# A gated linear-attention and feed-forward kernel: the last stage's steps in another order

## The chip, the cores and the metric

The kernel runs on one core of one Trainium2 chip. The metric is the device time of one execution in microseconds (us), here as the median of several runs. Beside it stands one profiled execution, whose trace gives the start and duration of every instruction on the engines PE (matrix), DVE (vector), ACT (scalar), POOL (GpSimd) and on the DMA queue that SP (SyncE) feeds.

## The reference

The input `x` has 2048 rows of 640 values. Two branches are computed from it and mixed row by row with a sigmoid gate.

```python
x = A_x
g = _sigmoid((x * gate_w).sum(-1, keepdims=True))
# branch A: 32 heads of 20; q, k, v from x @ wqkv
pq = einsum("bhsd,hdf->bhsf", q, w_phi);  pk = einsum("bhsd,hdf->bhsf", k, w_phi)
phi_q = concat([softmax(pq), softmax(-pq)]);  phi_k = concat([softmax(pk), softmax(-pk)])
kv = einsum("bhsf,bhsd->bhfd", phi_k, v);  z = einsum("bhsf->bhf", phi_k)
num = einsum("bhqf,bhfd->bhqd", phi_q, kv);  den = einsum("bhqf,bhf->bhq", phi_q, z) + 1e-6
a = (num / den) @ wo
# branch B: dense
b = silu(x @ w1) @ w2
return g * a + (1 - g) * b
```

## The kernel before

Products are made from operands that are split in a high part and a low part (`split`: ACT rounds a tile into its high part, then DVE or POOL subtracts it from the original), so most matrix products are three passes, listed in `PASSES`. The work is in three stages.

Stage 1 computes keys and values of 16 row tiles of 128 and sums `kv` and `z`. Stage 2 is the dense branch, in four blocks of 512 rows; its results, times 1 - g, go to the DRAM buffer `fb_d` (`acc_mm` is the last products of one of five output chunks, `acc_out` the DVE product into a tile `o` and its store). At the end of stage 2 the first four query tiles (rows 1536 to 2047) are already processed up to their feature maps. Stage 3, the last stage, handles the rest of the queries and all outputs. It works on eight pairs of tiles (256 rows), in the order `PB`; a pair is called u = 0 to 7.

For one query tile t the functions are, in order:

- `q_mm`: 30 matmuls project the tile into PSUM (`pq`).
- `q_logits`: DVE takes maximum and minimum of each head and subtracts (lines 410, 411 and twice 417), then ACT takes the exponential of 128x1280 values (line 776, tile `eq`).
- `q_norm`: POOL multiplies `eq` by the broadcast `z` (line 790, tile `ez`). `q_sum`: DVE sums `eq` over each head (line 780).
- `q_norm_sum`: DVE sums `ez` (line 793). `q_small`: five small instructions make the weights of each head from both sums and the gate (lines 801 to 820; DVE, for the first four tiles partly POOL).
- `q_mul`: POOL multiplies `eq` by these weights (line 826).

For a pair u: `t_all` transposes both tiles' `eq` on PE (line 963, `pT`) and copies them with ACT to `fT`; `n_mm` multiplies by the `kv` weights (line 1033, `pn`), three matmul groups; `n_out` makes the high part on ACT and the low part on DVE (`oT`); `w_mm(u, m0, n)` loads the dense result from `fb_d` into a tile `y` and multiplies `oT` by `wo` (line 1071, `pa`); `w_out` adds `y` and stores to `out`. Adding is done from a copy: ACT copies `pa` to `pac` (`w_copy`, line 1083), POOL adds (line 1094). For the last pair DVE adds straight from PSUM (line 1096). The five output chunks of a pair are taken in three groups, (0, 2), (2, 2) and (4, 1).

The transposes, `pn` and `pa` share four PSUM banks in turn (`single`), so a group waits until what stood in its bank four groups earlier is copied out. `pq` has two PSUM tiles of its own; they lie where the dense branch's banks were.

The inputs of stage 3's tiles come in 18 pieces (three per pair: 128x512, 128x512, 128x256). `x_next(k)` splits the next k pieces (ACT cast, then POOL subtract, both recorded with line 120 or 122) and issues the load of the piece four further on (line 216, tile `xrb`). The loads share four buffers, so piece p + 4 is loaded only when piece p is split.

Step u of stage 3 (function `step`, u = 1 to 6) handles the query tiles numbered a = 2u - 2, b = 2u - 1 and c = 2u; tiles a and b together are pair u + 1, which the next step transposes. In the first step a is tile 0, b is tile 1, c is tile 2. `inorder(PE, DVE, ACT, POOL)` around the stage makes the order in which the calls are written the order on each of these engines. SP's order of loads and stores is set by the scheduler from the order of the program. After the six steps `last_steps` transposes pair 7 and finishes the outputs of pairs 6 and 7.

Of the kernel before, what the change touches and what calls it, by code (L numbers as in the profile page):

```python
# [25 lines left out]
NP = S // 256  # L26
# [35 lines left out]
def mix_kernel(ctx: ExitStack, tc: tile.TileContext, xT, wqT, wkc, wkr, wv, bd, bdc, cst, wo, w1, w1r, w2, out):  # L62
# [729 lines left out]
    def q_norm_sum(t):  # L792
        nc.vector.tensor_reduce(Q[t]["sm"][:, 2 * H : 4 * H], groups(Q[t]["ez"]), axis=AX.X, op=ALU.add)  # L793

    def q_parts(t):

        s, sm = sums[t], Q[t]["sm"]
        w, parts = sm[:, 2 * H : 4 * H], halves(sm[:, 4 * H : 6 * H])
        first, other = halves(w)[:, :, 0], halves(s)[:, :, ::-1]
        if t // 4 == NB - 1:  # L800
            nc.gpsimd.tensor_tensor(first, sm[:, 4 * H : 5 * H], first, op=ALU.add)
            nc.gpsimd.tensor_tensor(parts, halves(w), other, op=ALU.mult)
        else:
            nc.vector.scalar_tensor_tensor(first, halves(s)[:, :, 0], 1e-6, first, op0=ALU.mult, op1=ALU.add)
            nc.vector.tensor_tensor(parts, halves(w), other, op=ALU.mult)

    def q_inv(t):
        sm = Q[t]["sm"]
        r = sm[:, :H]
        nc.vector.tensor_reduce(r, halves(sm[:, 4 * H : 6 * H]), axis=AX.X, op=ALU.add)  # L810
        nc.vector.reciprocal(r, r)

    def q_weights(t):
        s, sm = sums[t], Q[t]["sm"]
        w = sm[:, 2 * H : 4 * H]
        rb = sm[:, :H][:, :, None].to_broadcast([P, H, 2])
        if t // 4 == NB - 1:
            nc.gpsimd.tensor_tensor(halves(w), halves(sm[:, 6 * H :])[:, :, ::-1], rb, op=ALU.mult)
        else:
            nc.vector.scalar_tensor_tensor(  # L820
                halves(w), halves(s)[:, :, ::-1], g[:, t : t + 1], rb, op0=ALU.mult, op1=ALU.mult
            )
# [160 lines left out]
    with inorder(PE, DVE, ACT, POOL):  # L983
        q_open(t, q_proj(t))
        q_norm(t - 1)
        xb_split(2)
        acc_mm(0)
        q_feat(t)
        q_norm_sum(t - 1)
        q_parts(t - 1)  # L990
        acc_out(0)
        q_inv(t - 1)
        q_weights(t - 1)
        q_mul(t - 1)
        q_sum(t)
        q_norm(t)
        acc_mm(1)
        acc_out(1)
        acc_mm(2)
        acc_out(2)  # L1000
        for i in range(4):
            t_mm(0, i, bank)
            t_out(0, i)
        q_norm_sum(t)
        q_parts(t)
        acc_mm(3)
        acc_out(3)
        q_inv(t)
        q_weights(t)
        q_mul(t)  # L1010
        acc_mm(4)
        acc_out(4)

    closed("psf", "fp")
    tb = opened("tb", reuse_waits="tile")
# [68 lines left out]
        ws[u, m0] = y, a, n, cols  # L1084

    def w_out(u, m0):
        if u < NP - 1:
            w_copy(u, m0)
        w_add(u, m0)

    def w_add(u, m0):
        y, pa, n, cols = ws.pop((u, m0))
        if u < NP - 1:
            nc.gpsimd.tensor_tensor(y[:, :n], pa, y[:, :n], op=ALU.add)
        else:
            nc.vector.tensor_tensor(y[:, :n], pa[:, :n], y[:, :n], op=ALU.add)
        nc.sync.dma_start(out[m0 * P : (m0 + n) * P, cols].rearrange("(m p) s -> p m s", p=P), y[:, :n])
# [46 lines left out]
    def step(u):  # L1144
        a, b, c = 2 * u - 2, 2 * u - 1, 2 * u
        t_all(u, range(3))
        on(a, q_norm_sum, q_small, q_mul)
        if u == 1:
            x_next(2)
        on(b, q_mm)  # L1150
        t_all(u, range(3, 6))
        x_next(3)
        w_mm(u - 1, 0, 2)
        on(b, q_logits, q_norm)
        w_out(u - 1, 0)
        n_all(u)
        on(b, q_sum)
        n_out(u, range(3))
        on(b, q_norm_sum, q_small, q_mul)
        on(c, q_mm)  # L1160
        w_mm(u - 1, 2, 2)
        w_copy(u - 1, 2)
        on(c, q_logits)
        w_mm(u - 1, 4, 1)
        w_copy(u - 1, 4)
        w_add(u - 1, 2)
        on(c, q_sum, q_norm)
        w_add(u - 1, 4)

    def last_steps(u):  # L1170
        v = u + 1
        t_all(v, range(3))
        w_mm(u, 0, 2)
        t_all(v, range(3, 6))
        w_out(u, 0)
        w_mm(u, 2, 2)
        w_out(u, 2)
        n_all(v)
        n_out(v, range(3))
        w_mm(u, 4, 1)  # L1180
        w_out(u, 4)
        for m0, n in ((0, 2), (2, 2), (4, 1)):
            w_mm(v, m0, n)
            w_out(v, m0)

    with inorder(PE, DVE, ACT, POOL):
        t_all(0, range(4, 6))
        for gp in range(2):
            n_mm(0, gp)
        on(0, q_mm)  # L1190
        n_mm(0, 2)
        n_out(0, range(2))
        stack(WOR, wor[:GW, :D], raw("wor_h").bitcast(F32R)[:GW, :D], 2)
        for p in range(5, 7):
            x_ahead(p)
        x_next(2)
        on(0, q_logits)
        n_out(0, range(2, 3))
        on(0, q_sum, q_norm)
        for u in range(1, NP - 1):  # L1200
            step(u)
        last_steps(NP - 2)
# [65 lines left out]
```

## Time and profile before

| | |
|---|---|
| median of 3 runs | 759.42 us (758.81 to 761.13) |
| the profiled execution's own time | 759.67 us |
| its span, from the first to the last instruction | 757.9 us |
| PE busy | 746.7 us, 99% of the span |
| DVE, ACT, POOL busy | 343.8, 264.9, 262.2 us (45%, 35%, 35%) |
| stage 3 in the span | from about 578 us to the end |
| granted TensorE clock | full (1.0) |

The span lies inside the profiled time; 1.8 us are outside it. PE's busy time is the sum of its matmuls with modelled ends; idle time of PE is what the listings of waits and the timeline show in square brackets ("[2.08 <-POOL eq L826]": 2.08 us idle, ended by that POOL instruction). Starts are in us from the span's beginning.

### The profile page before, as it was taken

What the parts mean: (1) busy time and instruction counts of PE and PEld (TensorE: products, weight loads), DVE (VectorE), ACT (ScalarE), POOL (GpSimd) and SP (SyncE); (2) the same over time, 40 slices, a digit from 0 to 9 for tenths busy, and PEclk for the clock granted to TensorE, in tenths of its full rate; (3) what the DMA queues carried; (4) which work ended last, traced back from release to release, by engine and by line L of the source; (5) the groups of instructions that cost most, each with busy time, mean ns of one, the idle gap of its engine ahead of it and who ended that gap; (6) DMA issues with size and microseconds to landing.
All of it is one profiled execution on the core that took longest, in us unless ns stands there. A gap on an engine that the chain in (4) does not pass through costs nothing.

```text
span 757.9 us, 10463 instructions
## 1 busy us (share of the span) xinstructions
PE 746.7 (99%) x4187; PEld 649.1 (86%) x4187; DVE 343.8 (45%) x610; ACT 264.9 (35%) x481; POOL 262.2 (35%) x163
## 2 busy tenths in 40 slices
PE   8999999999999999999999999999999989999988
PEld 7888888888888888888888888888987989999987
DVE  5676666676651221012211122132477577676622
ACT  5444443346552311122111222133443543434331
POOL 2488777767100000000000000001167677766541
PEclk9999999999999999999999999999999999999999
DMA  7111111103660120002200015022003223111122
GB/s 257 51 54 53 53 53 53 59 29 99 194 193 1 58 95 1 1 0 72 84 0 1 1 54 170 17 71 87 15 1 120 94 81 98 56 57 56 57 81 81
DMA packets 35499, 50.38 MB, mean 66 GB/s; under 512 B 3544, under 2 KB 23272, under 8 KB 35450
## 3 DMA queue, kind: packets, MB, share of 16 engines
q1 hardware_dynamic: 35162, 49.19, 20.6%
q8 instruction: 33, 0.54, 0.3%
q10 hardware_dynamic: 288, 0.51, 0.2%
q14 instruction: 16, 0.13, 0.1%
HBM read 38.58 MB, written 11.11 MB: 66 GB/s over the span
## 4 chain that ended last, share of the span: by engine, by line
PE 91%; DVE 3%; POOL 2%; ACT 1%; DMA 1%; issue 1%; SPq 0%; POOLq 0%; DVEq 0%
PE acc L697 23%; PE ph L515 23%; PE kvp L468 16%; PE pa L1071 8%; PE pq L426 8%; PE kv L438 2%; PE pn L1033 2%; PE pT L963 2%; PE kvp L531 2%; PE kvp L327 1%; PE kvq L327 1%; PE pwk L316 1%; DVE sm L793 1%; POOL eq L826 1%; PE pwq L236 1%
## 5 line engine op out<-in xcount | busy, mean ns | idle before, releaser
L122 POOL TENSOR_TENSOR xb<-xrb,xb 128x512 fp32r<-128x512 f32 (+1 forms) x18 | 20.1, 1138 | 322.8 <-PE pwq L236 322.1
L697 PE MATMUL acc<-u,w 128*128 128x512 f32 x480 | 114.2, 391 | 0.2 <-DVE u L122 0.2
L122 DVE TENSOR_TENSOR u<-ph,u 128x512 fp32r<-128x512 f32 x48 | 33.2, 691 | 175.1 <-ACT u L120 175.0
L697 PEld LDWEIGHTS acc<-u,w 128*128 128x128 f32 x480 | 89.6, 188 | 19.2 <-DVE u L122 0.6
L515 PE MATMUL ph<-xf,w 128*128 128x512 f32 x420 | 99.4, 389 | 0.0
L517 ACT ACTIVATE ph<-ph 128x512 f32<-128x512 f32 x48 | 27.9, 582 | 190.1 <-PE ph L515 190.1
L468 PE MATMUL kvp<-wh,xa 128*128 128x500 f32 (+1 forms) x420 | 93.3, 358 | 0.0
L515 PEld LDWEIGHTS ph<-xf,w 128*128 128x128 f32 x420 | 78.8, 188 | 16.3
L468 PEld LDWEIGHTS kvp<-wh,xa 128*128 128x128 f32 x420 | 71.5, 188 | 10.0
L1071 PE MATMUL pa<-oT,wo 128*128 128x256 f32 x600 | 77.8, 283 | 1.3 <-ACT pac L1083 1.3
L1071 PEld LDWEIGHTS pa<-oT,wo 128*128 128x128 f32 x600 | 74.1, 189 | 2.5 <-ACT pac L1083 1.8
L697 PE MATMUL acc<-u,f 128*128 128x512 f32 x300 | 71.8, 390 | 0.0
L515 PE MATMUL ph<-xf,f 128*128 128x512 f32 x300 | 71.3, 389 | 0.0
L515 PEld LDWEIGHTS ph<-xf,f 128*128 128x128 f32 x300 | 56.3, 188 | 11.7
L697 PEld LDWEIGHTS acc<-u,f 128*128 128x128 f32 x300 | 56.2, 188 | 11.6
L790 POOL TENSOR_TENSOR ez<-eq,zbc 128x1280 f32<-128x1280 f32 x16 | 47.2, 2948 | 35.6 <-ACT eq L776 35.6
L122 POOL TENSOR_TENSOR ph<-ek,ph 128x1280 fp32r<-128x1280 f32 x16 | 47.4, 2964 | 28.3 <-ACT ph L120 28.3
L426 PE MATMUL pq<-wq,xb 128*128 128x320 f32 x360 | 55.9, 312 | 1.2 <-DVE o L945 1.2
L426 PEld LDWEIGHTS pq<-wq,xb 128*128 128x128 f32 x360 | 52.8, 188 | 3.6 <-DVE o L945 1.7
L826 POOL TENSOR_TENSOR eq<-eq,sm 128x1280 f32<-128x1280 f32 x16 | 37.9, 2368 | 32.2 <-DVE sm L820 27.1
L468 PE MATMUL kvp<-wl,xa 128*128 128x500 f32 (+1 forms) x210 | 47.6, 356 | 0.0
L496 POOL TENSOR_TENSOR ek<-ek,st 128x1280 f32<-128x1280 f32 x16 | 37.9, 2369 | 9.2 <-issue 6.1
(154 smaller groups left out, 1028.9 us busy)
## 6 DMA issues: line engine op xcount, KB each, us to landing
wr<-w SPq DMA_DIRECT2D x26, 320.0 KB, 3.2
xrf<-xT SPq DMA_DIRECT2D x20, 256.0 KB, 3.6
fb_d<-o SPq DMA_DIRECT2D x20, 256.0 KB, 2.3
y<-fb_d SPq DMA_DIRECT2D x16, 256.0 KB, 2.9
out<-y SPq DMA_DIRECT2D x16, 256.0 KB, 2.3
xra<-xT SPq DMA_DIRECT2D x14, 256.0 KB, 2.6
xrb<-xT SPq DMA_DIRECT2D x12, 256.0 KB, 2.7
wo<-wo SPq DMA_DIRECT2D x5, 320.0 KB, 2.9
```

The lines of the kernel that those rows point to most:

```text
L122: eng.tensor_tensor(lo, src, hi.bitcast(F32), op=ALU.subtract)
L327: nc.tensor.matmul(kv_cols(t, lo, hi), x_of(t)[c][:, hx, :], WKV[hw][:, c, lo:hi], start=(opens and hx == 0 and hw == 0), stop=(c == NC - ...
L426: nc.tensor.matmul(dst, xt[c][:, hx, :], w[:, c, hw, lo : lo + n], start=first, stop=(hx == 1 and c == NC - 1))
L438: nc.tensor.matmul(kvt[i // 2][: KF + 1, i % 2], vs[t % VB][:, i, : KF + 1], ph[:, :, ks[i] : ks[i] + P], start=(t == 0 and i % 2 == 0), s ...
L468: nc.tensor.matmul(kv_cols(t, lo, hi), xt[c][:, hx, :], WKV[hw][:, c, lo:hi], start=(n == 0), stop=(n == 3 * NC - 1), skip_group_check=True,)
L496: nc.gpsimd.tensor_tensor(groups(e), groups(e), spread(st[:, 1, :]), op=ALU.mult)
L515: nc.tensor.matmul(ph, lhs, rhs, start=(n == 0), stop=(n == len(todo) - 1))
L517: nc.scalar.activation(hs, ph, AF.Silu)
L697: nc.tensor.matmul(acc[m], lhs, rhs, start=(f == order[0] and n == 0), stop=(f == order[-1] and n == len(todo) - 1))
L790: nc.gpsimd.tensor_tensor(ez, Q[t]["e"], zbc, op=ALU.mult)
L826: nc.gpsimd.tensor_tensor(groups(q["e"]), groups(q["e"]), spread(q["sm"][:, 2 * H : 4 * H]), op=ALU.mult)
L1071: nc.tensor.matmul(pa[:, a, :], WO[:, c, hw, ds] if c < NG else WOR[:, ds], o[:, ho, c, :] if c < NG else o[:GW, 0, c, :], start=(k == 0), ...
```

## The change

Three things are changed, all in the order of calls around stage 3, and one in who adds.

1. At the end of the dense branch the last two outputs (`acc_mm`/`acc_out` 3 and 4) are written ahead of the remaining steps of the fourth query tile.
2. At the start of stage 3 all three `n_mm` groups of pair 0 stand ahead of the first `q_mm`. In step 1 one piece of input is split where two were; in every step `x_next(3)` stands behind `w_out(u - 1, 0)`, so behind tile b's exponential, and not ahead of `w_mm(u - 1, 0, 2)`.
3. In `last_steps` the groups of `w_mm` of pair 6 stand ahead of, between and behind the transposes of pair 7, all ahead of `n_all`. Pair 6 is added on DVE straight from PSUM, as pair 7 is.

```diff
         for i in range(4):
             t_mm(0, i, bank)
             t_out(0, i)
-        q_norm_sum(t)
-        q_parts(t)
         acc_mm(3)
         acc_out(3)
-        q_inv(t)
-        q_weights(t)
-        q_mul(t)
         acc_mm(4)
         acc_out(4)
+        q_norm_sum(t)
+        q_small(t)
+        q_mul(t)
@@
     def w_out(u, m0):
-        if u < NP - 1:
+        if u < NP - 2:
             w_copy(u, m0)
         w_add(u, m0)
@@ w_add
-        if u < NP - 1:
+        if u < NP - 2:
             nc.gpsimd.tensor_tensor(y[:, :n], pa, y[:, :n], op=ALU.add)
@@ step
         on(a, q_norm_sum, q_small, q_mul)
-        if u == 1:
-            x_next(2)
         on(b, q_mm)
         t_all(u, range(3, 6))
-        x_next(3)
+        if u == 1:
+            x_next(1)
         w_mm(u - 1, 0, 2)
         on(b, q_logits, q_norm)
         w_out(u - 1, 0)
+        x_next(3)
         n_all(u)
@@
     def last_steps(u):
         v = u + 1
+        w_mm(u, 0, 2)
+        w_out(u, 0)
         t_all(v, range(3))
-        w_mm(u, 0, 2)
-        t_all(v, range(3, 6))
-        w_out(u, 0)
         w_mm(u, 2, 2)
         w_out(u, 2)
+        t_all(v, range(3, 6))
+        w_mm(u, 4, 1)
+        w_out(u, 4)
         n_all(v)
         n_out(v, range(3))
-        w_mm(u, 4, 1)
-        w_out(u, 4)
         for m0, n in ((0, 2), (2, 2), (4, 1)):
@@
         t_all(0, range(4, 6))
-        for gp in range(2):
-            n_mm(0, gp)
+        n_all(0)
         on(0, q_mm)
-        n_mm(0, 2)
-        n_out(0, range(2))
+        n_out(0, range(3))
         stack(WOR, wor[:GW, :D], raw("wor_h").bitcast(F32R)[:GW, :D], 2)
         for p in range(5, 7):
             x_ahead(p)
         x_next(2)
         on(0, q_logits)
-        n_out(0, range(2, 3))
-        on(0, q_sum, q_norm)
+        on(0, q_norm, q_sum)
```

What this does to the engines is shown at three places. The first is DVE at the end of the dense branch. `o` is an output chunk's product, line 793 is the fourth query tile's sum of `ez`, lines 810 and 811 belong to its `q_inv`. Before:

```order
L793 TENSOR_REDUCE sm_4245<-ez_4284 128x64
L945 TENSOR_TENSOR o_3_4348<-acc_3_3476,G_3_3613 128x512
L810 TENSOR_REDUCE sm_4245<-sm_4245 128x32
L811 RECIPROCAL sm_4245<-sm_4245 128x32
L945 TENSOR_TENSOR o_4_4364<-acc_4_3477,G_3_3613 128x512
```

After, in the same place:

```order
L945 TENSOR_TENSOR o_3_4345<-acc_3_3476,G_3_3613 128x512
L945 TENSOR_TENSOR o_4_4357<-acc_4_3477,G_3_3613 128x512
L793 TENSOR_REDUCE sm_4245<-ez_4284 128x64
L810 TENSOR_REDUCE sm_4245<-sm_4245 128x32
L811 RECIPROCAL sm_4245<-sm_4245 128x32
```

Both products now come ahead of the sum, and nothing of the tile's small steps stands between them.

The second place is step 1, on ACT and on POOL. On ACT, `xb` are the casts of input pieces (the middle number is the chunk 0, 2 or 4), `fT` the copies of transposes, `eq` the exponential of tile b, `pac` the copy of the first `pa`. Before, on ACT:

```order
L120 CAST xb_4_4505<-xrb_4_4452 128x256
L120 CAST xb_0_4510<-xrb_0_4454 128x512
L979 COPY fT_2_4496<-pT_3_4549 120x512
L979 COPY fT_4_4563<-pT_4_4554 120x512
L979 COPY fT_4_4563<-pT_5_4559 80x256
L120 CAST xb_2_4566<-xrb_2_4459 128x512
L120 CAST xb_4_4571<-xrb_4_4464 128x256
L120 CAST xb_0_4576<-xrb_0_4508 128x512
L776 ACTIVATE eq_4548<-eq_4548 128x1280
L1083 COPY pac_0_4623<-pa_0_4583 128x512
```

After, on ACT:

```order
L979 COPY fT_2_4496<-pT_3_4539 120x512
L979 COPY fT_4_4553<-pT_4_4544 120x512
L979 COPY fT_4_4553<-pT_5_4549 80x256
L120 CAST xb_4_4556<-xrb_4_4456 128x256
L776 ACTIVATE eq_4538<-eq_4538 128x1280
L1081 COPY pac_0_4603<-pa_0_4563 128x512
L120 CAST xb_0_4607<-xrb_0_4458 128x512
L120 CAST xb_2_4612<-xrb_2_4463 128x512
L120 CAST xb_4_4617<-xrb_4_4468 128x256
```

One cast instead of five stands ahead of tile b's exponential, three follow it, and the fifth is left to the next step. On POOL in the same step, from the end of tile 0 (`eq_4439` before, `eq_4444` after) to the end of tile 1 (`eq_4548`, `eq_4538`), before:

```order
L826 TENSOR_TENSOR eq_4439<-eq_4439,sm_4437 128x1280
L122 TENSOR_TENSOR xb_4_4505<-xrb_4_4452,xb_4_4505 128x256
L122 TENSOR_TENSOR xb_0_4510<-xrb_0_4454,xb_0_4510 128x512
L122 TENSOR_TENSOR xb_2_4566<-xrb_2_4459,xb_2_4566 128x512
L122 TENSOR_TENSOR xb_4_4571<-xrb_4_4464,xb_4_4571 128x256
L122 TENSOR_TENSOR xb_0_4576<-xrb_0_4508,xb_0_4576 128x512
L790 TENSOR_TENSOR ez_4621<-eq_4548,zbc 128x1280
L1094 TENSOR_TENSOR y_0_4581<-pac_0_4623,y_0_4581 128x512
L826 TENSOR_TENSOR eq_4548<-eq_4548,sm_4546 128x1280
```

After, on POOL:

```order
L826 TENSOR_TENSOR eq_4444<-eq_4444,sm_4442 128x1280
L122 TENSOR_TENSOR xb_4_4556<-xrb_4_4456,xb_4_4556 128x256
L790 TENSOR_TENSOR ez_4601<-eq_4538,zbc 128x1280
L1092 TENSOR_TENSOR y_0_4561<-pac_0_4603,y_0_4561 128x512
L122 TENSOR_TENSOR xb_0_4607<-xrb_0_4458,xb_0_4607 128x512
L122 TENSOR_TENSOR xb_2_4612<-xrb_2_4463,xb_2_4612 128x512
L122 TENSOR_TENSOR xb_4_4617<-xrb_4_4468,xb_4_4617 128x256
L826 TENSOR_TENSOR eq_4538<-eq_4538,sm_4536 128x1280
```

The three subtractions stand now between the sum `y` and tile b's last product, where before no subtraction stood.

The third place is PE at the start of `last_steps`. `pT` are transposes of pair 7 (of tile a, `eq_5764`, and tile b, `eq_5895`), `pa_0` the first output group of pair 6. Before:

```order
L963 MATMUL pT_0_6053<-ident,eq_5764 120x128 x2
L963 MATMUL pT_0_6053<-ident,eq_5895 120x128 x2
L963 MATMUL pT_1_6058<-ident,eq_5764 120x128 x2
L963 MATMUL pT_1_6058<-ident,eq_5895 120x128 x2
L963 MATMUL pT_2_6063<-ident,eq_5764 120x128 x2
L963 MATMUL pT_2_6063<-ident,eq_5895 120x128 x2
L1071 MATMUL pa_0_6075<-oT_5959,wo 128x256 x15
L1071 MATMUL pa_0_6075<-oT_5959,wor_s 128x256
L1071 MATMUL pa_0_6075<-oT_5959,wo 128x256 x15
L1071 MATMUL pa_0_6075<-oT_5959,wor_s 128x256
L963 MATMUL pT_3_6108<-ident,eq_5764 120x128 x2
```

After:

```order
L1069 MATMUL pa_0_6055<-oT_5959,wo 128x256 x15
L1069 MATMUL pa_0_6055<-oT_5959,wor_s 128x256
L1069 MATMUL pa_0_6055<-oT_5959,wo 128x256 x15
L1069 MATMUL pa_0_6055<-oT_5959,wor_s 128x256
L963 MATMUL pT_0_6090<-ident,eq_5764 120x128 x2
L963 MATMUL pT_0_6090<-ident,eq_5895 120x128 x2
L963 MATMUL pT_1_6095<-ident,eq_5764 120x128 x2
L963 MATMUL pT_1_6095<-ident,eq_5895 120x128 x2
L963 MATMUL pT_2_6100<-ident,eq_5764 120x128 x2
L963 MATMUL pT_2_6100<-ident,eq_5895 120x128 x2
L1069 MATMUL pa_2_6112<-oT_5959,wo 128x256 x15
```

The first output group is ahead of the transposes that need both tiles, and the second group follows three transposes where before it followed all six. The third group, which stood behind `pn` of pair 7, is now ahead of it.

## The prediction, made before the changed kernel ran

> **What bounds the kernel now.** I read the waits of PE first, because PE is busy for 99% of the span, and only its idle time can be given back as long as its work stays the same. In the window from 560 us on, this is all that PE waited for in stage 3 (columns: who waited, for whom, total us, times, longest):
>
> ```profile
> PE pT L963 <- POOL eq L826: 3.0, 2, 2.1
> PE pa L1071 <- ACT pac L1083: 1.3, 1, 1.3
> PE pq L426 <- DVE o L945: 1.2, 1, 1.2
> ```
>
> Four waits, 5.5 us. Next I looked for their places in PE's timeline (start, us, what, in brackets the idle time before and its releaser):
>
> ```profile
> 578.40 1.95 PE L1033 MATMUL pn<-fT,kvw 120*64 120x256 f32 x16
> 581.57 4.66 PE L426 MATMUL pq<-wq,xb 128*128 128x320 f32 x30 [1.22 <-DVE o L945]
> 586.16 1.09 PE L1033 MATMUL pn<-fT,kvw 120*64 120x256 f32 x8
> 587.17 1.53 PE L963 MATMUL pT<-ident,eq 128*120 128x128 f32 x12
> 588.46 4.64 PE L426 MATMUL pq<-wq,xb 128*128 128x320 f32 x30
> ...
> 597.92 2.81 PE L1033 MATMUL pn<-fT,kvw 120*64 120x256 f32 x24
> 600.66 4.67 PE L426 MATMUL pq<-wq,xb 128*128 128x320 f32 x30
> ...
> 611.14 0.38 PE L963 MATMUL pT<-ident,eq 128*120 128x128 f32 x2
> 613.61 1.31 PE L963 MATMUL pT<-ident,eq 128*120 128x128 f32 x10 [2.08 <-POOL eq L826]
> 614.67 4.65 PE L426 MATMUL pq<-wq,xb 128*128 128x320 f32 x30
> ...
> 637.10 1.48 PE L963 MATMUL pT<-ident,eq 128*120 128x128 f32 x12
> ...
> 727.36 0.38 PE L963 MATMUL pT<-ident,eq 128*120 128x128 f32 x2
> 728.65 1.31 PE L963 MATMUL pT<-ident,eq 128*120 128x128 f32 x10 [0.91 <-POOL eq L826]
> 729.72 2.03 PE L1071 MATMUL pa<-oT,wo 128*128 128x256 f32 x15
> ...
> 733.61 1.26 PE L963 MATMUL pT<-ident,eq 128*120 128x128 f32 x10
> 736.12 2.04 PE L1071 MATMUL pa<-oT,wo 128*128 128x256 f32 x15 [1.25 <-ACT pac L1083]
> ...
> 742.84 2.06 PE L1071 MATMUL pa<-oT,wo 128*128 128x256 f32 x15
> ```
>
> Two waits are in the first 35 us of stage 3, two in the last 30; steps 2 to 5 between them show none. So the change is worth what happens at four places. I take start-to-start distances, since the listed ends are modelled: 30 `pq` matmuls 4.59 us (581.57 to 586.16), 24 `pn` 2.74 (597.92 to 600.66), 12 transposes 1.29 (587.17 to 588.46), 10 transposes 1.06 (613.61 to 614.67).
>
> **First place: the first `pq`.** It waited 1.22 us for the last dense output `o`, which gives its PSUM bank free. On DVE this product now stands ahead of the sum at line 793, so it is done right behind its matmuls, some 2 us before `pq` asks. Also the third `pn` group (8 matmuls, 586.16 to 587.17) comes ahead of `pq`. So: three `pn` groups from 578.40, 2.74 us, `pq` from 581.14 to 585.73, and the next transposes at 585.73 and not 587.17. PE has gained 1.44 us there, but tile 0's projection ends only 0.43 us earlier (586.16 to 585.73), and that is what the serial chain of tiles 0 and 1 feels. The fourth tile's weights come up to half a us later because line 793 now follows both products; its transposes have more slack than that, so I cost it at nothing.
>
> **Second place: the 2.08 us wait of step 1.** The chain that ended last shows tile 0 (first fence), the timeline shows tile 1 (then DVE, POOL, ACT):
>
> ```profile
> 589.31 1.28 ACT eq L776
> ...
> 590.66 2.97 POOL ez L790
> ...
> 593.65 1.50 DVE sm L793
> ```
>
> ```profile
> 598.70 0.81 DVE L417 TENSOR_TENSOR eq<-mmq,pq 128x640 f32<-128x640 f32 x1
> ...
> 608.13 1.48 DVE L793 TENSOR_REDUCE sm<-ez 128x64 f32<-128x1280 f32 x1
> ```
>
> ```profile
> 599.35 3.93 POOL L122 TENSOR_TENSOR xb<-xrb,xb 128x256 fp32r<-128x256 f32 x4
> ...
> 607.83 1.32 POOL L1094 TENSOR_TENSOR y<-pac,y 128x512 f32<-128x512 f32 x1
> 611.20 2.36 POOL L826 TENSOR_TENSOR eq<-eq,sm 128x1280 f32<-128x1280 f32 x1 [2.05 <-DVE sm L820]
> ...
> 623.84 3.20 POOL L122 TENSOR_TENSOR xb<-xrb,xb 128x512 fp32r<-128x512 f32 x3
> ...
> 633.07 2.37 POOL L826 TENSOR_TENSOR eq<-eq,sm 128x1280 f32<-128x1280 f32 x1 [1.85 <-DVE sm L820]
> ```
>
> ```profile
> 602.98 0.62 ACT L120 CAST xb<-xrb 128x512 fp32r<-128x512 f32 x1 [7.25 <-DMA xrb<-xT]
> 603.51 1.27 ACT L776 ACTIVATE eq<-eq 128x1280 f32<-128x1280 f32 x1
> ...
> 621.02 1.46 ACT L120 CAST xb<-xrb 128x512 fp32r<-128x512 f32 x3
> ```
>
> On SP's queue the loads of input pieces begin here:
>
> ```profile
> 585.90 19.48 SPq L216 DMA_DIRECT2D xrb<-xT  x9
> ```
>
> DVE had tile 1's logits ready at 598.70 + 0.81 = 599.51, but the exponential began at 603.51: ahead of it on ACT stood a cast that waited 7.25 us for its load, which in turn could be issued only when POOL had split the piece four before it (the splits from 599.35). After the change that cast is in the next step and three others stand behind the exponential; their buffers are those of pieces split ahead of tile 0's exponential, so their loads are among the first of these nine, some 10 us ahead. So the exponential starts at 599.51 - 0.43 = 599.08, 4.43 us earlier.
>
> What follows is now longer. POOL: exponential done at 600.35, `ez` 2.97, `y` 1.32, three splits 3.20 (the row at 623.84): free at 607.8. DVE: before, line 793 started 4.62 us behind the exponential's start and `q_mul` 3.07 behind that (608.13, 611.20). Three casts of 1.46 us now stand on ACT ahead of the copies `n_out` that line 793 follows. In full that gives 599.08 + 4.62 + 1.46 + 3.07 = 608.2; if DVE's own queue hides a part, POOL's 607.8 is the bound. `q_mul` of 2.36 then ends between 610.2 and 610.6; I take 610.4, the middle, as both bounds are near. PE comes to these transposes 1.44 us earlier, at 609.70, and to tile 1's at 610.08. So about 0.3 us of wait stays, and PE goes on at 610.45 instead of 613.61: 3.2 us gained. With no wait at all `pq` of the next tile would start at 609.70 + 1.29 = 610.99 against 614.67, 3.7 us.
>
> The moved casts bring three subtractions on POOL and three loads on SP with them in each of steps 1 to 4. On POOL they stand ahead of tile b's `q_mul`. In step 2 before, it ran from 633.07 to 635.44, and PE asked from 637.10: 1.7 us of slack. Before, the same 3.20 us stood ahead of `ez`, so POOL has the same work to do ahead of `q_mul` and ends it at about the same time; only `ez` and `y` come earlier within it. On SP a store of `y` can stand behind loads that wait for POOL; the stores have a whole step of 24 us until their buffer is read again. Cost: nothing, covered by that slack.
>
> **Third and fourth place: the last steps.**
>
> ```profile
> 726.24 2.36 POOL L826 TENSOR_TENSOR eq<-eq,sm 128x1280 f32<-128x1280 f32 x1 [3.54 <-DVE sm L820]
> ```
>
> ```profile
> 741.85 0.69 DVE L1050 TENSOR_TENSOR oT<-pn,oT 128x512 fp32r<-128x512 f32 x1 [15.78 <-ACT oT L1042]
> ...
> 744.08 0.47 DVE L1052 SCALAR_TENSOR_TENSOR oT<-pn,stk,oT 120x256 fp32r<-120x256 f32 x1
> 748.95 0.69 DVE L1096 TENSOR_TENSOR y<-pa,y 128x512 f32<-128x512 f32 x1 [4.39 <-issue]
> ```
>
> Pair 7's weights are ready at 728.60. With the first output group of pair 6 ahead (3.89 us, 729.72 to 733.61), PE asks at 731.25: the wait goes, with 2.6 us to spare. From 727.36 to 729.72 the 12 transposes took 2.36 us, now 1.29: 1.07 gained. From 733.61 the last 10 took 2.51 us up to the next `pa`, whose bank ACT had still to copy out behind the transposes' copies; now DVE, idle for 15.78 us there, adds 0.69 us behind the group's end, under 1.29 us of transposes: 2.51 - 1.06 = 1.45 gained. Three ACT copies and three POOL adds go; neither was on the path but for that bank. What is uncovered: the third group of pair 6 no longer stands between `pn` and pair 7's first `pa`, which reads the fresh `oT`. Before, the last low part was ready at 744.55, 1.71 us behind the start of that group (742.84). The matmuls that need low parts come from the eleventh of sixteen on, so at the least nothing is lost; at the most, if the first matmul waited for all, 1.71. I take 0.1, near the lower end, since the high parts are wanted one after another. Third and fourth place: 1.07 + 1.45 - 0.1 = 2.4.
>
> **Sum.** 3.2 + 2.4 = 5.6 us off the profiled 759.67: 754.1. The median of the runs is 0.25 below the profiled one, so nothing is added for that.
>
> **A rule weighed.** Splits on POOL do not all take the same time (min, median, max in ns), and the slowest stood beside a DVE instruction with both tensors in SBUF:
>
> ```profile
> L122 POOL TENSOR_TENSOR xb<-xrb,xb x16: 722/1271/1876, 568.5 to 670.6; 128x512 fp32r<-128x512 f32 x10, 128x256 fp32r<-128x256 f32 x6
> ```
>
> ```profile
> 582.62 1.93 DVE L728 SCALAR_TENSOR_TENSOR wor_s<-wor,stk,wor_h 120x640 fp32r<-120x640 f32 x1
> ```
>
> If the two large splits in their new place took 1876 ns, `q_mul` would end 2 x 0.6 = 1.2 us later, and the gain be 4.4. I keep 1271: the DVE work beside the new place is what stood beside the row of 3.20. [...]
>
> **Rivals.** (1) The new waits are at their far ends: 1.2 us more on POOL or 1.6 more at pair 7's first `pa`. One gives 755.3 to 755.7, both 756.9. For it speaks that both places lose their cover, against it that the rows are single extremes. (2) The exponential of step 1 gains nothing, because the piece left ahead of it (or the three behind it, through the copies) still waits for its load. Then the 3.2 goes and 2.4 stays: 757.3. Against it: only one ACT wait on such a load is in the trace, and it was for a piece four behind a late split. (3) Slower: the splits now ahead of `q_mul` of tile b wait for loads in each of steps 1 to 4. POOL works in order, so a cast that waits 7.25 us, as the one above, holds `q_mul` up by as much, less 1.7 of slack: 5.5 us in each of four steps, 22 in all, against 5.6 gained: 776. It decides from about 3.1 us of wait in each step on (1.4 times four is 5.6). Against it: the loads are issued a step ahead.
>
> **How the numbers follow.** The forecast, 754.1, gets 0.70 with its own range of 753.2 (no wait left, 3.7 + 2.5, less the 0.25 of the median) to 755.0; rival 1 gets 0.17, rival 2 0.08, rival 3 0.05. The range from 753.0 to 756.9 leaves out rivals 2 and 3. A measurement can tell about 0.3%, 2.3 us, from no change, so faster means below 757.1: the first two cases and a part of rival 2, 0.89; same is 0.07, slower 0.04.
>
> **What would show it.** Right: no wait of `pq` for `o`; the ACT row of tile 1's exponential begins less than 0.1 us behind DVE's last subtraction; PE's wait for `eq` in step 1 under 0.6 us; no `eq` and no `pac` wait after 720 us. Wrong: an ACT row `xb` that waits for a load behind 600 us, waits for `eq` in steps 2 to 5, a wait of `pa` for `oT` over 1 us in the last 15 us, or a `y` load that DVE waits for.

## The result and the profile after

The changed kernel took 753.43 us in the median of six runs (752.93 to 754.42). The kernel before took 760.70 us in six runs (758.81 to 761.13), of which the three runs known beforehand, with a median of 759.42, are a part. The ratio is 0.9911, with a 95% interval of 0.9899 to 0.9924. The forecast was 754.1, in a range of 753.0 to 756.9. The profiled execution took 753.52 us (before 759.67), and its span is 751.7 us (before 757.9).

From 560 us on, this is all that PE waits for now (who, for whom, total us, times, longest):

```profile
PE pT L963 <- POOL eq L826: 0.6, 1, 0.6
PE acc L697 <- DVE u L122: 0.2, 1, 0.2
```

The second row belongs to the dense branch and stands in the list of before as well. Of the four waits in stage 3, 5.5 us, one of 0.57 is left. PE's busy time hardly changed: 746.7 us before, 745.9 now.

PE's timeline at the start of stage 3 and in the last steps (start, us, what, the idle time before it):

```profile
578.25 2.81 PE L1031 MATMUL pn<-fT,kvw 120*64 120x256 f32 x24
580.99 4.66 PE L426 MATMUL pq<-wq,xb 128*128 128x320 f32 x30
585.49 1.47 PE L963 MATMUL pT<-ident,eq 128*120 128x128 f32 x12
...
609.14 0.38 PE L963 MATMUL pT<-ident,eq 128*120 128x128 f32 x2
610.09 1.31 PE L963 MATMUL pT<-ident,eq 128*120 128x128 f32 x10 [0.57 <-POOL eq L826]
611.16 4.65 PE L426 MATMUL pq<-wq,xb 128*128 128x320 f32 x30
615.64 1.25 PE L963 MATMUL pT<-ident,eq 128*120 128x128 f32 x10
...
727.67 1.48 PE L963 MATMUL pT<-ident,eq 128*120 128x128 f32 x12
728.90 2.04 PE L1069 MATMUL pa<-oT,wo 128*128 128x256 f32 x15
...
732.81 1.26 PE L963 MATMUL pT<-ident,eq 128*120 128x128 f32 x10
733.83 2.04 PE L1069 MATMUL pa<-oT,wo 128*128 128x256 f32 x15
...
738.66 2.13 PE L1069 MATMUL pa<-oT,wo 128*128 128x256 f32 x15
...
740.75 1.94 PE L1069 MATMUL pa<-oT,wo 128*128 128x256 f32 x15
...
748.22 0.28 PE L1069 MATMUL pa<-oT,wor_s 120*128 120x256 f32 x1
```

From the first `pn` to the `pq` behind tile 1's transposes PE needed 614.67 - 578.40 = 36.27 us before and needs 611.16 - 578.25 = 32.91 now: 3.36 gained. The first 12 transposes of the last steps (727.36 to 729.72 before) went from 2.36 to 1.23 us, the last 10 (733.61 to 736.12) from 2.51 to 1.02.

The engines that fed tile 1's transposes, ACT first, then DVE, then POOL:

```profile
598.95 1.27 ACT L776 ACTIVATE eq<-eq 128x1280 f32<-128x1280 f32 x1 [5.47 <-DVE eq L417]
```

```profile
598.10 0.81 DVE L417 TENSOR_TENSOR eq<-mmq,pq 128x640 f32<-128x640 f32 x1
...
607.12 0.28 DVE L820 SCALAR_TENSOR_TENSOR sm<-pq,g,sm 128x64 f32<-128x64 f32 x1
```

```profile
604.47 3.24 POOL L122 TENSOR_TENSOR xb<-xrb,xb 128x512 fp32r<-128x512 f32 x3
607.64 2.39 POOL L826 TENSOR_TENSOR eq<-eq,sm 128x1280 f32<-128x1280 f32 x1
```

The exponential starts at 598.95, 0.04 us behind DVE's last subtraction (598.91). The wait named beside it is now for DVE and no longer for a load. DVE's weights end at 607.40, and POOL's splits let `q_mul` begin at 607.64, so both queues end within a quarter of a microsecond of each other, POOL last.

### The profile page after: what moved, and what is told of

Same layout as the page of the kernel before. It is cut to its first block, busy times and chain, and to the rows that moved or that the text cites. A ratio compares the mean times of both kernels' runs of the same rounds, so it can differ in the third digit from the quotient of the medians.

```text
span 751.7 us, 10464 instructions
## 1 busy us (share of the span) xinstructions
PE 745.9 (99%) x4187; PEld 649.2 (86%) x4187; DVE 345.1 (46%) x613; ACT 262.9 (35%) x478; POOL 258.8 (34%) x160
## 4 chain that ended last, share of the span: by engine, by line
PE 95%; POOL 2%; DVE 1%; ACT 1%; issue 1%; DMA 1%; SPq 0%; POOLq 0%
PE acc L697 25%; PE ph L515 23%; PE kvp L468 16%; PE pa L1069 9%; PE pq L426 8%; PE pn L1031 3%; PE kv L438 3%; PE pT L963 2%; PE kvp L531 2%; PE kvp L327 1%; PE kvq L327 1%; PE pwk L316 1%; PE pwq L236 1%; POOL eq L826 1%; DMA wvr<-wv 1%
## 5 line engine op out<-in xcount | busy, mean ns | idle before, releaser
L468 PEld LDWEIGHTS kvp<-wl,xa 128*128 128x128 f32 x210 | 36.3, 189 | 5.5
```

The costliest lines, as they stand in the source:

```text
L468: nc.tensor.matmul(kv_cols(t, lo, hi), xt[c][:, hx, :], WKV[hw][:, c, lo:hi], start=(n == 0), stop=(n == 3 * NC - 1), skip_group_check=True,)
```

## Experiments

The start of stage 3 varies between executions: in the traces below the first `pn` begins between 577.98 and 580.25 us, although nothing ahead of it was changed by that much. The two late ones, tail_only (580.25) and pq_first (579.63), are late from their first 10 us on, in which PE's matmuls ran slowly for longer. This one of tail_only took 0.51 us, the same one in the kernel before (at 7.28 us) 0.32 and in pq_first (at 7.98 us) 0.50:

```profile
8.54 0.51 PE L327 MATMUL kvp<-wh,xa 128*128 128x360 f32 x1
```

Matmuls of this shape take 0.32 or 0.33 us from 5.54 us on in the kernel before, and still 0.50 or 0.51 from 6.09 to 8.84 us in tail_only, but the mean clock given for tail_only is 1.0 all the same. So an execution can be some 2 us longer without a sign of it in its mean clock, and beside the times I use the length of stage 3 in the trace, from the start of the first `pn` to the start of the last `pa<-oT,wor_s`. In the kernel before, that last row is

```profile
754.31 0.28 PE L1071 MATMUL pa<-oT,wor_s 120*128 120x256 f32 x1
```

| kernel | first `pn` | last `pa` | length, us | against | difference |
|---|---|---|---|---|---|
| before | 578.40 | 754.31 | 175.91 | | |
| changed | 578.25 | 748.22 | 169.97 | before | -5.94 |
| start_only | 578.32 | 755.18 | 176.86 | before | +0.95 |
| splits_only | 577.98 | 751.38 | 173.40 | before | -2.51 |
| tail_only | 580.25 | 753.43 | 173.18 | before | -2.73 |
| after_copy6 | 578.82 | 748.81 | 169.99 | changed | +0.02 |
| splits_early | 578.39 | 749.43 | 171.04 | changed | +1.07 |
| pq_first | 579.63 | 749.15 | 169.52 | changed | -0.45 |
| splits_late | 578.35 | 748.00 | 169.65 | changed | -0.32 |
| wait_2 | 578.32 | 751.49 | 173.17 | changed | +3.20 |
| wait_3h | 578.18 | 753.61 | 175.43 | changed | +5.46 |

These lengths are of one execution each. The ratios are all against the kernel before, run on the same chip.

The theory was that of the prediction: each part of the change takes away a wait of PE, and the parts add. The rivals were that a part only moves its wait elsewhere, that the number of pieces split in step 1 and not their place is what counts, and that adding on DVE and not the order frees the bank in the last steps.

### start_only: the first place alone

The kernel before, with the dense outputs ahead of the sum at line 793 and with the new start of stage 3; `step` and `last_steps` as before.

```diff
-        q_norm_sum(t)
-        q_parts(t)
         acc_mm(3)
         acc_out(3)
-        q_inv(t)
-        q_weights(t)
-        q_mul(t)
         acc_mm(4)
         acc_out(4)
+        q_norm_sum(t)
+        q_small(t)
+        q_mul(t)
@@
         t_all(0, range(4, 6))
-        for gp in range(2):
-            n_mm(0, gp)
+        n_all(0)
         on(0, q_mm)
-        n_mm(0, 2)
-        n_out(0, range(2))
+        n_out(0, range(3))
...
-        n_out(0, range(2, 3))
-        on(0, q_sum, q_norm)
+        on(0, q_norm, q_sum)
```

> The kernel before with the first part alone: the last two dense outputs taken at once, all three pn groups of pair 0 ahead of the first pq. Theory (the wait of step 1 is set by the serial chain of tiles 0 and 1, and that chain only feels when tile 0's projection ends): the 1.22 us wait of pq for o goes, PE comes to step 1's transposes about 1.5 us earlier, but tile 1's weights only about 0.5 us earlier, so the 2.08 us wait for eq grows to about 3.0 and the kernel gains about 0.5 us. Rival (the gains add, each wait is its own): the wait for eq stays at 2.1 and the kernel gains 1.4 us.

Measured: 760.43 us (758.47 to 762.51), ratio 1.0004 (0.9993 to 1.0015). PE's and ACT's rows of step 1:

```profile
604.50 2.04 PE L1069 MATMUL pa<-oT,wo 128*128 128x256 f32 x15 [0.83 <-ACT pac L1081]
...
612.81 2.27 PE L963 MATMUL pT<-ident,eq 128*120 128x128 f32 x10 [2.14 <-POOL eq L826]
614.73 5.40 PE L426 MATMUL pq<-wq,xb 128*128 128x320 f32 x30
619.97 0.27 PE L963 MATMUL pT<-ident,eq 128*120 128x128 f32 x1
```

```profile
602.19 0.62 ACT L120 CAST xb<-xrb 128x512 fp32r<-128x512 f32 x1 [7.77 <-DMA xrb<-xT]
602.71 1.27 ACT L776 ACTIVATE eq<-eq 128x1280 f32<-128x1280 f32 x1
603.88 0.57 ACT L1081 COPY pac<-pa 128x512 f32<-128x512 f32 x1
```

The wait of `pq` for `o` is gone. The time that PE gained came back in step 1 as waiting, at two places: 0.83 us for the copy `pac`, which stands on ACT behind the late exponential, and 2.14 us for `eq`, 2.97 together, where one wait of 3.0 had been expected. PE then lost more: the ten transposes took 612.81 to 614.73, 1.92 us, and `pq` 5.24 (to 619.97), where the changed kernel has 1.07 and 4.48. That is 1.61 us, and the granted clock shows why (window, busy time by engine, then PEclk):

```profile
610.00:613.00 3.00, 0.86 (x8) 0.62 (x8) 3.00 (x5) 0.00 (x0) 2.60 (x2) 1.00 0.33 92
613.00:616.00 3.00, 3.00 (x15) 3.00 (x15) 1.66 (x2) 2.79 (x5) 2.44 (x2) 0.50 0.26 88
616.00:620.00 4.00, 4.00 (x28) 3.99 (x28) 2.35 (x6) 0.20 (x1) 2.18 (x2) 0.95 0.33 98
```

For some 3.4 us behind the wait the clock was half: 3.0 us at a mean of 0.50, and 0.4 us more by the mean of 0.95 over the next four. Without these 1.61 us the stage would be 175.25, 0.66 less than before, near the 0.5 expected; as it ran, this part alone gained nothing.

### splits_only: the second place alone

The kernel before with the new `step`, nothing else.

```diff
         on(a, q_norm_sum, q_small, q_mul)
-        if u == 1:
-            x_next(2)
         on(b, q_mm)
         t_all(u, range(3, 6))
-        x_next(3)
+        if u == 1:
+            x_next(1)
         w_mm(u - 1, 0, 2)
         on(b, q_logits, q_norm)
         w_out(u - 1, 0)
+        x_next(3)
         n_all(u)
```

> The kernel before with the input splits moved and nothing else. Theory: tile 1's exponential starts right behind DVE's last subtraction, near 599.5 instead of 603.5, its weights are ready near 610.6, before PE asks at 611.5, so the wait of 2.08 us goes in full and the kernel gains 2.1 to 2.4 us; the other three waits stay. Rival (the splits are hidden, step 1's wait is bound by POOL and DVE work that stays): gain under 1 us, and the wait stays over 1 us.

Measured: 757.15 us (756.47 to 759.98), ratio 0.9972 (0.9961 to 0.9984); the stage is 2.51 us shorter. The transposes of step 1 run through:

```profile
610.45 1.48 PE L963 MATMUL pT<-ident,eq 128*120 128x128 f32 x12
```

The other three waits (1.2, 1.3 and 0.9 us) stay. So this part is worth its own wait and 0.4 more, and needs neither of the other two parts.

### tail_only: the third and fourth place alone

The kernel before with the new `last_steps`, and pair 6 added on DVE.

```diff
     def w_out(u, m0):
-        if u < NP - 1:
+        if u < NP - 2:
             w_copy(u, m0)
         w_add(u, m0)
@@ w_add
-        if u < NP - 1:
+        if u < NP - 2:
             nc.gpsimd.tensor_tensor(y[:, :n], pa, y[:, :n], op=ALU.add)
@@ last_steps
+        w_mm(u, 0, 2)
+        w_out(u, 0)
         t_all(v, range(3))
-        w_mm(u, 0, 2)
-        t_all(v, range(3, 6))
-        w_out(u, 0)
         w_mm(u, 2, 2)
         w_out(u, 2)
+        t_all(v, range(3, 6))
+        w_mm(u, 4, 1)
+        w_out(u, 4)
         n_all(v)
         n_out(v, range(3))
-        w_mm(u, 4, 1)
-        w_out(u, 4)
```

> The kernel before with the new order of the last steps and pair 6 added on DVE, nothing else. Theory: the two waits after 720 us go, 2.5 us gained; the waits at 581 and 613 us stay at 1.2 and 2.1. Rival (pair 7's first pa, which now follows pn at once, waits for the fresh oT): 0.8 to 1.0 us gained, with a wait for oT of about 1.6 us.

Measured: 758.27 us (756.21 to 761.72), ratio 0.9979 (0.9965 to 0.9992); the stage is 2.73 us shorter, and both waits behind 720 us are gone, while those of 2.1 and 1.2 us stay. With start_only counted without the clock's 1.61 us, the three parts add: 0.66 + 2.51 + 2.73 = 5.90, against 5.94 for the whole change.

### after_copy6: pair 6 copied by ACT and added by POOL again

The changed kernel with the old way of adding in the new order.

```diff
     def w_out(u, m0):
-        if u < NP - 2:
+        if u < NP - 1:
             w_copy(u, m0)
@@ w_add
-        if u < NP - 2:
+        if u < NP - 1:
             nc.gpsimd.tensor_tensor(y[:, :n], pa, y[:, :n], op=ALU.add)
```

> The changed kernel, with pair 6 again copied by ACT and added on POOL, in the new order of the last steps. Theory: the order alone frees the bank in time, since ACT's copy of 0.59 us now stands ahead of the transposes' copies and lies under 1.29 us of transposes: within 0.3 us of the changed kernel, no wait of pa for pac. Rival (adding on DVE is what removed the wait, as the prediction put it): the pac wait is back at about 1.2 us, and the kernel is 1.2 to 1.5 us slower than the changed one.

Measured: 753.26 us (752.99 to 754.17), ratio 0.9913 (0.99 to 0.9927); the stage is the changed kernel's to 0.02 us, with the same two rows of waits. ACT's rows show why:

```profile
733.65 0.58 ACT L1081 COPY pac<-pa 128x512 f32<-128x512 f32 x1 [3.09 <-PE pa L1069]
734.14 1.33 ACT L979 COPY fT<-pT 120x512 f32<-120x512 f32 x3
```

In the new order the copy stands ahead of the copies of the transposes. Before, it stood behind them and began only at 735.47:

```profile
735.47 0.60 ACT L1083 COPY pac<-pa 128x512 f32<-128x512 f32 x1
```

So the new order is enough to take the bank's wait away, and in it who adds makes no difference. Whether adding on DVE in the old order would have been enough too was not run.

### splits_early: the three pieces ahead of the exponential again

The changed kernel, with `x_next(3)` where it stood before in every step, but still one piece and not two in step 1.

```diff
         if u == 1:
             x_next(1)
+        x_next(3)
         w_mm(u - 1, 0, 2)
         on(b, q_logits, q_norm)
         w_out(u - 1, 0)
-        x_next(3)
         n_all(u)
```

> The changed kernel with x_next(3) put back ahead of w_mm(u - 1, 0, 2); in step 1 one piece and three, so four pieces ahead of tile 1's exponential where the kernel before had five. Theory: none of these four waits for a load, so the exponential still starts near 599.0; but the four subtractions stand ahead of ez on POOL, ez starts about 2 us later, tile 1's weights come about 1 us later, and the wait of step 1 grows from 0.57 to about 1.6 us: 1.0 us slower than the changed kernel. Rival (any cast ahead of the exponential holds it up): the exponential starts 3 to 4 us later, the kernel is about 4 us slower. Other rival (place is worth nothing, only the count): no difference.

Measured: 754.24 us (754.04 to 754.95), ratio 0.9918 (0.9904 to 0.9931); the stage is 1.07 us longer than the changed kernel's. POOL and PE in step 1:

```profile
598.88 3.95 POOL L122 TENSOR_TENSOR xb<-xrb,xb 128x256 fp32r<-128x256 f32 x4
602.79 2.94 POOL L790 TENSOR_TENSOR ez<-eq,zbc 128x1280 f32<-128x1280 f32 x1
...
608.84 2.36 POOL L826 TENSOR_TENSOR eq<-eq,sm 128x1280 f32<-128x1280 f32 x1 [1.86 <-DVE sm L820]
```

```profile
611.25 0.98 PE L963 MATMUL pT<-ident,eq 128*120 128x128 f32 x7 [1.58 <-POOL eq L826]
```

The exponential is as early as in the changed kernel (599.09), since the fifth piece, whose load came late, is no longer ahead of it. But POOL's four splits now hold `ez` up to 602.79, while `eq` was ready at 600.36 (1.27 us behind 599.09), and DVE then lets POOL wait 1.86. So the count frees the exponential, and the place frees POOL. With the new start of stage 3 in all three, PE waits in step 1 for 2.97 us with the old place and count (start_only, both waits), for 1.58 with the new count alone, and for 0.57 with both.

### pq_first: the projection ahead of the third `pn` group again

The changed kernel with the old start of stage 3; the dense outputs stay ahead.

```diff
         t_all(0, range(4, 6))
-        n_all(0)
+        for gp in range(2):
+            n_mm(0, gp)
         on(0, q_mm)
-        n_out(0, range(3))
+        n_mm(0, 2)
+        n_out(0, range(2))
...
-        on(0, q_norm, q_sum)
+        n_out(0, range(2, 3))
+        on(0, q_sum, q_norm)
```

> The changed kernel with the start of the last stage as before: two pn groups, the first pq, the third pn group. Theory (the chain of tiles 0 and 1 is what step 1 waits for): pq starts about 0.7 us earlier, near 580.3, since o is already done; the chain and tile 1's weights come 0.7 us earlier, and the 0.57 us wait of step 1 falls to 0.1 or less: 0.5 to 0.7 us faster than the changed kernel. Rival (step 1's wait is set by POOL's splits, whose loads and casts don't hang on pq): the wait stays and the time is the same.

Measured: 754.45 us (752.59 to 754.98), ratio 0.9912 (0.9896 to 0.9927). No wait of PE is left in stage 3:

```profile
579.63 1.95 PE L1031 MATMUL pn<-fT,kvw 120*64 120x256 f32 x16
581.51 4.67 PE L426 MATMUL pq<-wq,xb 128*128 128x320 f32 x30
```

`pq` follows 1.88 us behind the first `pn` with no wait, so the order of the dense outputs alone removed the wait for `o`. In the changed kernel it follows 2.74 us behind (578.25 to 580.99), so tile 0's projection begins 0.86 us sooner here, and that is what `q_mul` of step 1 lacked. The stage is 0.45 us shorter than the changed kernel's, where 0.5 to 0.7 had been expected. The total times of the two can't be told apart.

### splits_late: the three pieces of step 1 behind tile 1's weights

The changed kernel; only in step 1 `x_next(3)` goes behind `q_mul` of tile b.

```diff
         w_out(u - 1, 0)
-        x_next(3)
+        if u > 1:
+            x_next(3)
         n_all(u)
         on(b, q_sum)
         n_out(u, range(3))
         on(b, q_norm_sum, q_small, q_mul)
+        if u == 1:
+            x_next(3)
```

> The changed kernel with x_next(3) of step 1 alone put behind tile 1's last product (q_mul). Theory: neither the casts on ACT nor the subtractions on POOL stand ahead of tile 1's weights, which come about 1.3 us earlier, near 608.7; the wait of 0.57 us goes, 0.6 to 0.8 us gained; tile 2's ez comes about 1.5 us later behind the subtractions, which step 2's slack of over 2 us takes, with at most 0.3 us of wait at its end. Rival (the delay is handed on): a wait for eq of 0.6 us or more appears in step 2 or 3 and the time is the same or longer.

Measured: 753.38 us (752.7 to 754.83), ratio 0.991 (0.9894 to 0.9926).

```profile
606.75 2.37 POOL L826 TENSOR_TENSOR eq<-eq,sm 128x1280 f32<-128x1280 f32 x1 [2.11 <-DVE sm L820]
```

```profile
609.25 1.47 PE L963 MATMUL pT<-ident,eq 128*120 128x128 f32 x12
...
633.53 1.31 PE L963 MATMUL pT<-ident,eq 128*120 128x128 f32 x10 [0.25 <-POOL eq L826]
```

Without the casts and splits ahead, `q_mul` begins 0.89 us sooner and the wait of step 1 is gone. But the three splits now stand ahead of tile 2's `ez`, which begins at 613.52 where the changed kernel has 611.71. The delay is handed on: tile 3's `q_mul` ends at 633.47 (631.70 in the changed kernel), and step 2 gets a wait of 0.25, within the 0.3 that had been allowed for. The stage is 0.32 us shorter, less than the 0.6 to 0.8 expected; the total is the same within its interval.

### wait_2 and wait_3h: a longer wait made on purpose

To see whether the clock's fall in start_only hangs on the length of PE's wait, the changed kernel got one more POOL product in step 1, ahead of `q_mul` of tile b. It writes again what stands there, on 640 columns (wait_2) or all 1280 (wait_3h).

```diff
-        on(b, q_norm_sum, q_small, q_mul)
+        on(b, q_norm_sum, q_small)
+        if u == 1:
+            for lo, hi in [(0, 640)]:
+                nc.gpsimd.tensor_tensor(
+                    Q[QT[b]]["ez"][:, lo:hi], Q[QT[b]]["e"][:, lo:hi], zbc[:, lo:hi], op=ALU.mult
+                )
+        on(b, q_mul)
```

> The changed kernel with one extra POOL product of 128x640 in step 1, ahead of tile 1's q_mul (it writes again what stands there). It takes about 1.5 us, so the wait of step 1 goes from 0.57 to about 2.1 us, as long as in the kernel before. Theory (a wait of PE of some 2 us can make the granted clock fall to half for some 3.4 us, which costs 1.7 us more): 1.5 us slower than the changed kernel where the clock stays, 3.2 where it falls, and the clock falls in a part of the executions (mean clock 0.998), some 4 in 10, as in those of the kernel before. Rival (the falls come from elsewhere, or only from longer waits): no mean clock of 0.998, 1.5 us slower throughout.

> The same with the extra product over 128x1280, about 2.95 us, so that the wait of step 1 is about 3.5 us. Theory: the clock falls in most executions, more than 6 in 10, and then the kernel is 2.95 + 1.7 = 4.6 us slower than the changed one. Rival (falls do not hang on this wait): 2.95 us slower, with the clock as in the changed kernel.

Measured: wait_2 756.70 us (755.14 to 758.37), ratio 0.9949 (0.9936 to 0.9961); wait_3h 757.89 us (757.58 to 758.98), ratio 0.9967 (0.9955 to 0.9979). PE in wait_2, then its windows:

```profile
611.80 1.83 PE L963 MATMUL pT<-ident,eq 128*120 128x128 f32 x10 [2.20 <-POOL eq L826]
613.28 5.80 PE L426 MATMUL pq<-wq,xb 128*128 128x320 f32 x30
618.92 1.25 PE L963 MATMUL pT<-ident,eq 128*120 128x128 f32 x10
```

```profile
612.00:613.00 1.00, 1.00 (x9) 1.00 (x8) 1.00 (x1) 0.73 (x2) 1.00 (x2) 0.72 0.00 0
...
615.00:616.00 1.00, 1.00 (x6) 1.00 (x6) 0.12 (x1) 0.00 (x0) 1.00 (x2) 0.58 0.00 0
```

The same of wait_3h:

```profile
613.01 2.39 PE L963 MATMUL pT<-ident,eq 128*120 128x128 f32 x10 [3.55 <-POOL eq L826]
```

```profile
611.00:612.00 1.00, 0.00 (x0) 0.00 (x0) 0.40 (x1) 0.83 (x2) 1.00 (x1) 0.79 0.00 0
612.00:618.00 6.00, 4.99 (x21) 5.00 (x22) 2.01 (x2) 1.76 (x3) 5.73 (x4) 0.50 0.20 60
618.00:619.00 1.00, 1.00 (x8) 1.00 (x7) 0.93 (x3) 0.00 (x0) 0.00 (x0) 0.80 0.80 276
```

In wait_2 the wait grew by 1.63 us and the stage by 3.20. The rest is the clock: from 611.80 to 618.92 PE needed 7.12 us for what takes 5.55 in the changed kernel (610.09 to 615.64), 1.57 more. In wait_3h the wait grew by 2.98 and the stage by 5.46; PE works at half clock there from 613.01 to 618.40. The costs came as expected where the clock falls once (3.2 us in wait_2; 4.6 in wait_3h, whose median is 4.46 above the changed kernel's), but the fall came more often in wait_2 than the 4 in 10 expected, in five executions of six.

## Why the prediction was right, point by point

**First place.** As forecast, the wait for `o` is gone and PE comes to the transposes sooner: 7.24 us behind the first `pn` (578.25 to 585.49) against 8.77, 1.53 gained where 1.44 was forecast. The prediction counted the third `pn` group ahead of `pq` as a part of how this works, with tile 0 only 0.43 us earlier. pq_first showed that this part works against the gain: it delays tile 0's projection by 0.86 us, and costs 0.45 in the end.

**Second place.** The exponential was forecast for 599.08 and came at 598.95, and `q_mul` was to end between 610.2 and 610.6 and ended at 610.03. The bounds by DVE and by POOL did lie close together (607.40 and 607.64). The three casts on ACT, taken in full with 1.46 us, delayed line 793 by 0.91 only (604.48 is 5.53 us behind the exponential, where it was 4.62), so POOL was last. A wait of about 0.3 was forecast, and 0.57 is there, because PE came 0.56 us sooner to the two transposes before (609.14 against 609.70) and `q_mul` ended only 0.37 sooner than the 610.4 taken. 3.2 us were forecast and 3.36 measured: 1.53 at the first place, 1.51 from the wait (2.08 to 0.57), and 0.3 that the prediction had not seen. That last piece seems to have been a wait too short for the list. In the kernel before, `pac` was copied behind the late exponential, and PE's next group began as the copy ended:

```profile
604.68 0.57 ACT L1083 COPY pac<-pa 128x512 f32<-128x512 f32 x1
```

```profile
605.30 2.05 PE L1071 MATMUL pa<-oT,wo 128*128 128x256 f32 x15
```

The copy ended at 605.25. From `pq` at 600.66 to the two transposes at 611.14 PE needed 10.48 us; splits_only, where the exponential is early, needed 10.21 (600.24 to 610.45). In start_only, where PE came sooner still, the same place became the wait of 0.83 us.

**The moved splits.** They cost nothing in steps 2 to 5, as said: no wait of PE is listed there. In step 2 tile b's `q_mul` now ends at 631.70 and PE comes to the transposes at 633.58, so the slack of 1.7 us is still there, at 1.9. It was used up only in splits_late, which ends the same `q_mul` 1.8 us later.

**Third and fourth place.** 2.4 us were forecast as 1.07 + 1.45 - 0.1. The rows give 1.13 (2.36 to 1.23), 1.49 (2.51 to 1.02), and 0.07 lost where pair 7's first `pa` now follows `pn` (2.09 us from 738.66 to 740.75; before, the `pa` that followed `pn` took 2.02, from 742.84 to 744.86): 2.55. One step was narrower than what the runs show. It put the 1.45 down to DVE, whose sum of 0.69 us behind the group's end frees the bank; after_copy6 shows that ACT's copy does as well, once it is issued ahead of the copies of the transposes. The number held because either way the bank is free under 1.2 us of transposes.

**The sum.** 5.6 us were forecast, the stage gave 5.94, and the profiled time fell by 6.15; the other 0.2 us lie outside that length. The median fell by 7.3 us; what the two traces do not show of that is treated in the last section. The forecast counted from the profiled execution of before, at full clock, so the time came out nearer (753.43 against 754.1) than the gain of the medians did.

**The slow splits.** The three splits took 3.24 us in their new place, 3.20 in the old one, so the term of 1.2 us for slow splits rightly stayed out. Beside them on DVE stood for the most part the sum of line 793 and the small steps (604.48 to 607.40), and not, as the prediction had it, what stood beside the old row of 3.20 (623.84 to 627.04 in the kernel before: the end of line 417 and the sum of line 780). The 3.24 us show no delay by it. The slow case showed once more where it was before:

```profile
581.75 2.38 POOL L826 TENSOR_TENSOR eq<-eq,sm 128x1280 f32<-128x1280 f32 x1
584.08 3.10 POOL L122 TENSOR_TENSOR xb<-xrb,xb 128x512 fp32r<-128x512 f32 x2
```

```profile
583.00 1.81 DVE L728 SCALAR_TENSOR_TENSOR wor_s<-wor,stk,wor_h 120x640 fp32r<-120x640 f32 x1
```

The DVE instruction with two SBUF inputs ended at 584.81, 0.68 us behind the POOL product's end at 584.13, and the two splits that follow from 584.08 took 3.10 us, nearly as much as three in the new place. The same row of the kernel before ended 0.68 us behind its POOL product too (584.55 and 583.87), and its two splits took 3.11 us. That the DVE instruction is what slows them was not shown, as no run takes it away.

**The rivals.** Rival 1 would have shown 1.2 us more on POOL or 1.6 at pair 7's first `pa`; neither came. Rival 2 did not happen, as no cast of stage 3 waits for a load any more, and neither did rival 3, as steps 2 to 5 show no wait.

## What to carry to other kernels

An engine that works in the written order lets any instruction stand in the way of all behind it: in the kernel before, a cast of a piece whose load was late held an unrelated exponential up by 4 us (599.51 to 603.51), and the product behind it on another engine with it. Before such a step is moved, count for each of the queues what stands ahead of the late instruction, and expect the gain of one place to be spent at the next wait of the same chain, as in start_only, unless that is removed too. Where two parts of a change go against each other, try each alone: here two variants, pq_first and splits_late, are a little better in the trace, by 0.45 and 0.32 us, and too close to tell by the total time. They were not run together.

## What was not expected of the hardware

Behind waits of PE of 2.14 us (start_only) and 2.20 us (wait_2) its granted clock fell to half in the traces. In wait_2 it falls at about 612.44 (a mean of 0.72 in that microsecond, then 0.50) and is back at about 615.84 (a mean of 0.58 in that microsecond): 3.40 us. PE waited from 609.60 to 611.80, so the fall came 0.64 us after it had begun to work again. In wait_3h, with a wait of 3.55 us, the clock is half from about 611.58 to 618.40 (means of 0.79, 0.50 and 0.80), 6.82 us, twice as long, although PE worked again from 613.01. In start_only it lasted about 3.4 us behind a wait of 2.14.

It doesn't come in every execution. A fall of 3.4 us brings the mean clock of an execution to 0.998, as in the profiled ones of start_only and wait_2. Of wait_2's six executions five have that, and the sixth, at 1.0, is the fastest with 755.14 us; all five of wait_3h have 0.998 or 0.995. Six of start_only's twelve executions have 0.998 or less, and seven of tail_only's twelve, which keeps the wait of 2.1. Of the kernel before, whose longest wait is 2.08 us, 11 of the 29 executions beside the first four experiments have 0.997 or 0.998 and a median of 760.89 us, and the 18 others 759.08. No execution of the changed kernel has it (six, wait of 0.57), nor of splits_early (four, wait of 1.58), nor of after_copy6, pq_first and splits_late (five each). A fall costs some 1.6 to 1.8 us: 1.61 in start_only's trace, 1.57 in wait_2's, 1.81 between the two medians of the kernel before. One thing stays open: two of splits_only's twelve executions have 0.998 as well, though the longest wait in its trace is 1.3 us; neither of the two has a trace.

Why a wait of some 2 us does it in one execution and not in another is not shown. The waits of 2.14, 2.20 and 3.55 us come with a fall in their traces; the wait of 2.08 us in the traces of the kernel before and of tail_only does not, and the ten transposes behind it take the same 1.06 us in both (613.61 to 614.67 and 615.31 to 616.37), where they take 1.92 in start_only and 1.48 in wait_2 (611.80 to 613.28). These are five traces, of one execution each.

The falls are probably a part of why the median fell by more than the trace: the change removes the wait of 2.08, and the profiled execution of before, at 1.0, had no fall. That they are all of it is not shown. The six executions behind the 760.70 us have no clock on record, and of the 20 executions of before beside the later experiments nine took 760.14 to 761.34 us at a mean clock of 1.0; matmuls that run slowly for longer at the start, as in tail_only (0.51 us against 0.32), would look like that. From the lowest time to the lowest, 758.81 to 752.93 us, the gain is 5.88 us, near the trace's.
